# Decoding buffers moved to the memory that the global keys and values use later, and the decodings of the third block drawn together

## Chip, core and metric

One core of one Trainium2 chip runs the whole program. The time is device microseconds of one execution, and the span is what the profile shows from the first to the last instruction. The engines are named as the profile names them: PE (TensorE matmuls), PEld (its weight loads), DVE (VectorE), ACT (ScalarE), POOL (GpSimd) and SP (SyncE, which issues the transfers).

## What is computed

Attention with a local and a global part, then two feed-forward layers on the same 2304 tokens of width 512. Cut to what matters:

```python
s_g = scale * q_g @ k_all^T              # 32 global queries of a head see all 544 keys
out_g = softmax(s_g) @ v_all
s_l = scale * q_l @ [k_g, k_l]^T         # local: a window of 32 to each side, and the global keys
out_l = softmax(masked s_l) @ [v_g, v_l]
x = tokens of [out_g, out_l]             # 2304 x 512
x = elu(x @ w_in) @ w_out                # first layer, 512 -> 2048 -> 512
xn = x / rms(x) * rms_g                  # second layer, 512 -> 1536 -> 512
out = (silu(xn @ w_gate) * (xn @ w_val)) @ w_o2
```

The weights arrive as 64-bit floats. The kernel turns each word pair into a 32-bit float on ACT and DVE; this is what "decoding" means below.

## The kernel before

**Tiling.** The local tokens are four blocks of 512 (block 0 to block 3; the third block is block 2). `moe_block(b, slot)` runs the first layer for one block in 16 steps, j = 0 to 15. A step is `mm1` (12 matmuls into `h`, line 128), `act1` (ACT makes `e` from `h`, DVE finishes it, ACT copies a high part of `g`, line 135, and DVE makes its low part, line 136), and `mm2` for the `g` of the step before (12 matmuls into four `y`, line 142). `slot(j, part, h)` is called three times in a step and puts other work between the matmuls.

**Beside the steps of blocks 0 to 2** the local attention of the next block runs, one chunk of 128 tokens in four steps (`att_slot`): the scores `a_S` on PE (lines 209 to 219), the maximum `mx` on DVE (227) and the exponentials `E` on ACT (230), in the next step the transposes `a_T` (236), in the one after it `a_PV` (249) and `a_N`. The keys and queries of the next chunk (`load_kq`) are loaded once `a_S` has read the buffer, its values (`load_v`) once `a_PV` has.

**Decodings of the second layer's weights.** There are 18, each for 1 MiB of raw words. `w2_decode` (in part 2 of some steps of blocks 1 and 2) takes the oldest raw tile: ACT takes its absolute value into `dx` (line 79), DVE makes four passes over it (86 to 89), SP stores the result to `wT` in device memory (453), and `w2_load` (71) asks for the raw tile after next. There are two `raw` tiles (pool `decr`) and two `dx` tiles (pool `dec`). So decoding n waits for a load that is sent when decoding n-2 is done.

**Block 3** has the global attention beside it instead (`slot3`). `g_load_k(0)` loads the tile `gkq` (line 678, 1152 KB) and `g_load_v` two tiles `gvr` (685); `g_S` multiplies with them in step 0 (698), between `mm1` and `mm2`. Their pool is opened after the attention and decoding pools of blocks 0 to 2 have been closed and takes over their memory. In the kernel before, the two decoding pools are opened last in that group of pools (line 330).

**Order.** PE's order is the order of the code (`manual_schedule` for PE). A scheduler orders DVE, ACT and SP; each engine then runs its instructions in order, and a waiting instruction holds up all behind it on its engine.

Of the kernel before, what the change touches and what calls it, by code (L numbers as in the profile page):

```python
# [39 lines left out]
def fused_kernel(ctx: ExitStack, tc: tile.TileContext, kq, vl, gkq, gv, w_in, w_out, w_gate, w_val, w_o2, rms_g, consts, out):  # L40
# [91 lines left out]
    def act1(h, n, fn=None):  # L132
        e = (fn or elu)(h, n)
        g = moe.tile([P, 2, 512], F32R, tag="g", name="g", bufs=2)
        nc.scalar.copy(g[:, 0, :n], e[:, :n])  # L135
        nc.vector.tensor_tensor(out=g[:, 1, :n], in0=e[:, :n], in1=f(g[:, 0, :n]), op=ALU.subtract)  # L136
        return g
# [33 lines left out]


    with ExitStack() as ls:
        ac = ls.enter_context(tc.tile_pool(name="attc", bufs=1))
        ap_ = ls.enter_context(tc.tile_pool(name="attl", bufs=1))
        masks = ac.tile([P, 3, P], F32R, name="masks")
# [7 lines left out]
        def load_kq(u):  # L184
            if u < 16:
                if u < 4:
                    t = wpool.tile([P, 4, KC], F32, tag="w", name="kq0")
                else:
                    t = ap_.tile([P, 4, KC], F32, tag="kq", name="kq_")
                nc.sync.dma_start(out=t, in_=kq[u].rearrange("p (a n) -> p a n", a=4))  # L190
                kq_t[u] = t
# [87 lines left out]
        def att_slot(b, j, part):  # L279

            u, jj = 4 * (b + 1) + j // 4, j % 4
            if jj == 0 and part == 0:
                a_S(u, ATT2)
                a_E(u)
                load_kq(u + 1)
            if jj == 1 and part < 2:
                a_T(u, part, aps, "att")
            if jj == 2 and part == 0:
                a_PV(u, ATT2)
                a_N(u)  # L290
                load_v(u + 1)
# [35 lines left out]
            carry.append((ys, prev, t0, n))  # L327


        dec = {"t": ls.enter_context(tc.tile_pool(name="dec", bufs=2)), "r": ls.enter_context(tc.tile_pool(name="decr", bufs=2))}  # L330
        load_kq(0)
        mk = moe.tile([P, 3, P], F32, tag="e", name="mk", bufs=2)
        nc.sync.dma_start(out=ident, in_=consts[:, 3 * P:4 * P])
# [112 lines left out]
        def w2_decode():  # L446
            i = n_dec2[0]
            if i < 18:
                n_dec2[0] += 1
                raw = raws2.pop(0)  # L450
                t = dec_abs(dec["t"], raw, keep=True)
                dec_bits(t, raw)
                nc.sync.dma_start(out=wT[2 * i:2 * i + 2].rearrange("a p n -> p a n"), in_=t.rearrange("p (a n) -> p a n", a=2))
                w2_load()
# [15 lines left out]
        def slot12(b):  # L470
            def slot(j, part, h):
                g = act1(h, 512) if part == 0 else None
                att_slot(b, j, part)
                if part == 2:
                    if j % 2 or (b == 2 and j in (4, 10)):
                        w2_decode()
                return g

            return slot
# [429 lines left out]
```

## Time and profile before

| | us |
|---|---|
| median of 3 runs (lowest, highest) | 964.2 (962.63, 964.56) |
| the profiled execution's own time | 963.88 |
| its span | 962.1 |
| PE busy | 919.5 (96%) |
| DVE busy | 461.8 (48%) |
| ACT busy | 346.9 (36%) |
| DMA, mean over the span | 112 GB/s |

The page cuts the span into 40 slices and gives each engine's busy share of each. PE is at 90% or more in nearly all slices from the fifth on; the others are well below, DVE with its highest shares in the first third. The profiled execution stands 0.3 us under the median, so sums against its own time can be compared with the median as they are.

### The profile page before, as it was taken

Reading aid. Unit: us, or ns where it says so; the run is one execution under the profiler, and the core shown is the slowest. Engines: PE = TensorE matmul, PEld = TensorE weight load, DVE = VectorE, ACT = ScalarE, POOL = GpSimd, SP = SyncE. Lnnn points to the kernel's source line nnn. Section 1 sums busy time; section 2 is a strip of 40 time slices with the busy share of each in tenths; the row PEclk is TensorE's granted clock in tenths of the full one; section 3 lists DMA queues with packets and bytes.
Section 4 is the critical chain, followed back from the end, with each engine's and each line's share of the span. In section 5 each row is a group of like instructions: output and inputs, shape, how many; then the busy total and the mean of one; then the engine's idle time right before and its main releaser. Section 6 shows DMA issues by size and latency. Waiting matters only on the chain.

```text
span 962.1 us, 15714 instructions
## 1 busy us (share of the span) xinstructions
PE 919.5 (96%) x6738; PEld 769.7 (80%) x6738; DVE 461.8 (48%) x791; ACT 346.9 (36%) x627; POOL 17.9 (2%) x19
## 2 busy tenths in 40 slices
PE   6788899999999999599999999999999999999997
PEld 5666688888887887467788888888889999999996
DVE  4899953666656866434577313321332142141111
ACT  4566644433334344223465313121222232232111
POOL 0000000000000000000010100000000100100000
PEclk9989999999999999799999999999999999999999
DMA  9675441554465662533453200110011010000000
GB/s 362 243 293 197 171 163 45 185 176 173 170 240 179 233 244 89 218 133 131 183 171 111 77 0 1 33 44 1 1 33 44 1 33 33 1 1 33 1 1 33
DMA packets 34445, 107.77 MB, mean 112 GB/s; under 512 B 3016, under 2 KB 5704, under 8 KB 31816
## 3 DMA queue, kind: packets, MB, share of 16 engines
q1 hardware_dynamic: 34376, 106.77, 30.9%
q8 instruction: 53, 0.87, 0.4%
q14 instruction: 16, 0.13, 0.0%
HBM read 88.41 MB, written 18.35 MB: 111 GB/s over the span
## 4 chain that ended last, share of the span: by engine, by line
PE 82%; DVE 9%; DMA 3%; ACT 2%; issue 2%; SPq 0%; ACTq 0%; DVEq 0%
PE y L142 15%; PE pg L631 15%; PE pv L631 15%; PE y L637 15%; PE h L128 13%; DVE dx L89 2%; DVE dx L88 2%; PE ptp L236 2%; PE o L249 1%; PE yg L595 1%; PE s L219 1%; PE hg L579 1%; DMA kq<-in_kq 1%; PE s L214 1%; DVE wA L95 1%
## 5 line engine op out<-in xcount | busy, mean ns | idle before, releaser
L142 PE MATMUL y<-g,wA 128*128 128x512 f32 x768 | 201.4, 407 | 3.7 <-DVE g L136 3.4
L128 PE MATMUL h<-xT,wA 128*128 128x512 f32 x768 | 186.0, 391 | 1.3 <-DVE xT L274 1.3
L142 PEld LDWEIGHTS y<-g,wA 128*128 128x128 f32 x768 | 141.4, 192 | 37.3 <-DVE g L136 4.6
L128 PEld LDWEIGHTS h<-xT,wA 128*128 128x128 f32 x768 | 143.6, 188 | 31.9 <-DVE xT L274 1.5
L804 DVE TENSOR_TENSOR silu<-pv,silu 128x384 f32<-128x384 f32 (+1 forms) x60 | 36.6, 611 | 257.4 <-PE pv L631 251.3
L637 PE MATMUL y<-wB,p 128*128 128x512 f32 x612 | 149.0, 391 | 0.0
L637 PEld LDWEIGHTS y<-wB,p 128*128 128x128 f32 x612 | 114.5, 188 | 22.3
L803 ACT ACTIVATE silu<-pg 128x384 f32<-128x384 f32 (+1 forms) x60 | 32.0, 534 | 159.5 <-PE pg L631 159.3
L631 PE MATMUL pv<-xT,wB 128*128 128x384 f32 (+1 forms) x432 | 88.4, 353 | 0.0
L631 PEld LDWEIGHTS pv<-xT,wB 128*128 128x128 f32 x432 | 77.3, 188 | 5.6
L806 ACT CAST p<-silu 128x384 fp32r<-128x384 f32 (+1 forms) x60 | 33.3, 556 | 127.2 <-DVE silu L804 126.9
L135 ACT CAST g<-e 128x512 fp32r<-128x512 f32 x64 | 39.7, 621 | 72.6 <-DVE e L111 69.0
L109 ACT ACTIVATE e<-h 128x512 f32<-128x512 f32 x48 | 28.8, 600 | 94.8 <-PE h L128 87.5
L631 PE MATMUL pv<-xnB,wB 128*128 128x512 f32 (+1 forms) x288 | 61.5, 362 | 0.0
L631 PE MATMUL pg<-xT,wB 128*128 128x384 f32 (+1 forms) x288 | 60.1, 357 | 0.0
L631 PEld LDWEIGHTS pg<-xT,wB 128*128 128x128 f32 x288 | 52.2, 188 | 5.8 <-issue 0.5
L631 PEld LDWEIGHTS pv<-xnB,wB 128*128 128x128 f32 x288 | 52.2, 188 | 5.6
L110 DVE TENSOR_SCALAR e<-e 128x512 f32<-128x512 f32 x52 | 22.2, 428 | 70.9 <-ACT e L109 70.9
L807 DVE TENSOR_TENSOR p<-silu,p 128x384 fp32r<-128x384 f32 (+1 forms) x60 | 38.0, 633 | 35.5 <-ACT p L806 35.5
L136 DVE TENSOR_TENSOR g<-e,g 128x512 fp32r<-128x512 f32 x64 | 45.2, 706 | 17.4 <-ACT g L135 16.2
L79 ACT ACTIVATE dx<-raw 128x1024 f32<-128x1024 f32 x34 | 39.3, 1156 | 11.1 <-DVE wA L95 4.3
L230 ACT ACTIVATE E<-s,mx 128x128 f32<-128x128 f32 x128 | 34.9, 384 | 23.2 <-DVE mx L228 21.1
(179 smaller groups left out, 957.1 us busy)
## 6 DMA issues: line engine op xcount, KB each, us to landing
raw<-in_moe_w_out SPq DMA_DIRECT2D x14, 1024.0 KB, 5.3
wT<-dx SPq DMA_DIRECT2D x18, 512.0 KB, 3.9
wraw<-wT SPq DMA_DIRECT2D x18, 512.0 KB, 4.4
raw<-in_moe_w_in SPq DMA_DIRECT2D x8, 1024.0 KB, 7.0
raw<-in_moe_w_gate SPq DMA_DIRECT2D x6, 1024.0 KB, 7.8
raw<-in_moe_w_val SPq DMA_DIRECT2D x6, 1024.0 KB, 8.3
gvr<-in_gv SPq DMA_DIRECT2D x8, 640.0 KB, 4.5
gkq<-in_gkq SPq DMA_DIRECT2D x4, 1152.0 KB, 5.1
```

What stands on the lines that cost most here:

```text
L79: ins = nc.scalar.activation(x, f(words(raw)[:, :, 1]), AF.Abs)
L128: nc.tensor.matmul(h[:, :n], W1[c, G][:, ws, o:o + P], xT[c][:, xs, :n], start=(k == 0), stop=(k == 11))
L135: nc.scalar.copy(g[:, 0, :n], e[:, :n])
L136: nc.vector.tensor_tensor(out=g[:, 1, :n], in0=e[:, :n], in1=f(g[:, 0, :n]), op=ALU.subtract)
L142: nc.tensor.matmul(ys[dc][:, :n], W2[j][:, ws, dc * P:(dc + 1) * P], g[:, gs, :n], start=(j == 0 and k == 0), stop=(j == 15 and k == 2))
L230: nc.scalar.activation(e[par][:, pr, :], ss[par][:, pr, :], AF.Exp, bias=mx[:, par, pr:pr + 1], scale=SCALE)
L631: nc.tensor.matmul(ps[:, :n], W[c, G3][:, ws, o:o + P], xn[c][:, xs, :n], start=(k == 0), stop=(k == 11))
L637: nc.tensor.matmul(os_[t], p[:, pp, t * P:(t + 1) * P], Wo[j][:, ww, :], start=(j == 0 and k == 0), stop=(j == 11 and k == 2))
L803: nc.scalar.activation(s[:, :n], pg[:, :n], AF.Silu)
L804: nc.vector.tensor_tensor(out=s[:, :n], in0=pv[:, :n], in1=s[:, :n], op=ALU.mult)
L806: nc.scalar.copy(p[:, 0, :n], s[:, :n])
L807: nc.vector.tensor_tensor(out=p[:, 1, :n], in0=s[:, :n], in1=f(p[:, 0, :n]), op=ALU.subtract)
```

## The change

The pools of the decoding tiles are opened first in their group instead of last, so that the memory handed out first when the group is closed is theirs. In block 2, `w2_decode` is called in steps 0 to 4 and 6 to 10 instead of in the odd steps and in steps 4 and 10. Both make ten decodings in that block; block 1 stays as it was, with one in each odd step.

```diff
     with ExitStack() as ls:
+
+        dec = {"t": ls.enter_context(tc.tile_pool(name="dec", bufs=2)), "r": ls.enter_context(tc.tile_pool(name="decr", bufs=2))}
         ac = ls.enter_context(tc.tile_pool(name="attc", bufs=1))
...
-        dec = {"t": ls.enter_context(tc.tile_pool(name="dec", bufs=2)), "r": ls.enter_context(tc.tile_pool(name="decr", bufs=2))}
         load_kq(0)
...
                 if part == 2:
-                    if j % 2 or (b == 2 and j in (4, 10)):
+                    if (j % 2 if b == 1 else j < 12 and j % 6 != 5):
                         w2_decode()
```

PE's instructions keep their order. What moves stands on DVE, ACT and SP from the start of block 2 to the start of block 3. Lines 176 to 331 of the changed kernel are two lower than before and those behind them one lower, so that its 229, 230, 232 and 240 are the 227, 228, 230 and 238 of before.

DVE in step 4 of block 2, before. `e_3208` and `g_3212` belong to step 4, `mx_3259` to the chunk whose scores run in that step, `dx_3186` and `dx_3288` are decodings:

```order
L110 TENSOR_SCALAR e_3208<-e_3208 128x512
L89 SCALAR_TENSOR_TENSOR dx_3186<-raw_2912,dx_3186 128x1024
L111 SCALAR_TENSOR_TENSOR e_3208<-h_3195,e_3208 128x512
L227 TENSOR_REDUCE mx_3259<-s_3215 128x4
L136 TENSOR_TENSOR g_3212<-e_3208,g_3212 128x512
L227 TENSOR_REDUCE mx_3259<-s_3216 128x4
L228 TENSOR_SCALAR mx_3259<-mx_3259 128x4 x2
L86 TENSOR_SCALAR dx_3288<-dx_3288 128x1024
```

The same place after the change, where `e_3185` and `g_3189` belong to step 3, `e_3226` and `g_3230` to step 4, `dx_3163` and `dx_3204` to the decodings called in steps 2 and 3, and `mx_3277` to the same chunk:

```order
L89 SCALAR_TENSOR_TENSOR dx_3163<-raw_3030,dx_3163 128x1024
L111 SCALAR_TENSOR_TENSOR e_3185<-h_3172,e_3185 128x512
L136 TENSOR_TENSOR g_3189<-e_3185,g_3189 128x512
L86 TENSOR_SCALAR dx_3204<-dx_3204 128x1024
L87 TENSOR_SCALAR dx_3204<-dx_3204 128x1024
L110 TENSOR_SCALAR e_3226<-e_3226 128x512
L88 SCALAR_TENSOR_TENSOR dx_3204<-raw_3085,dx_3204 128x1024
L111 SCALAR_TENSOR_TENSOR e_3226<-h_3213,e_3226 128x512
L89 SCALAR_TENSOR_TENSOR dx_3204<-raw_3085,dx_3204 128x1024
L136 TENSOR_TENSOR g_3230<-e_3226,g_3230 128x512
L229 TENSOR_REDUCE mx_3277<-s_3233 128x4
```

Before, the first maximum stood ahead of `g` of its step; now a whole further decoding and the `g` stand ahead of both maxima.

ACT in steps 10 to 12 of block 2, before (`e_3713`, `e_3754` and `e_3845` are of steps 11, 12 and 13):

```order
L79 ACTIVATE dx_3691<-raw_3466 128x1024
L109 ACTIVATE e_3713<-h_3700 128x512
L135 CAST g_3717<-e_3713 128x512
L79 ACTIVATE dx_3732<-raw_3614 128x1024
L109 ACTIVATE e_3754<-h_3741 128x512
L135 CAST g_3758<-e_3754 128x512
```

And after (`e_3654`, `e_3736` and `e_3768` are of steps 10, 11 and 12):

```order
L79 ACTIVATE dx_3634<-raw_3484 128x1024
L135 CAST g_3605<-e_3601 128x512
L109 ACTIVATE e_3654<-h_3641 128x512
L135 CAST g_3658<-e_3654 128x512
L79 ACTIVATE dx_3716<-raw_3586 128x1024
L109 ACTIVATE e_3736<-h_3723 128x512
L135 CAST g_3740<-e_3736 128x512
L109 ACTIVATE e_3768<-h_3755 128x512
```

`dx_3716` is now the last decoding, ahead of the `e` of step 11, and none follows it; before, two more followed `dx_3732`, the last of them after step 15.

SP ahead of block 3, before:

```order
L71 DMA raw_3739<-in_moe2_w_out 128x2x512
L453 DMA wT_86<-dx_3878 128x2x512
L453 DMA wT_86<-dx_4022 128x2x512
L678 DMA gkq_4043<-in_gkq 128x2304
L685 DMA gvr_4045<-in_gv 128x1280
```

And after:

```order
L71 DMA raw_3586<-in_moe2_w_out 128x2x512
L202 DMA v__3702<-in_vl 128x2080
L454 DMA wT_86<-dx_3634 128x2x512
L454 DMA wT_86<-dx_3716 128x2x512
L679 DMA gkq_4043<-in_gkq 128x2304
```

The two stores ahead of `gkq` were those of the decodings called in steps 13 and 15 and are now those of steps 9 and 10.

## Rows read from the trace of the kernel before

**Rows 1.** The page, part 2: PE's busy tenths in 40 slices of the span.
```profile
PE   6788899999999999599999999999999999999997
```
**Rows 2.** Timeline of PE, end of block 2 and start of block 3: start us, us, instruction.
```profile
372.56 1.12 PE L249 MATMUL o<-v__3677,ET 128*32 128x65 f32 x64
...
384.37 2.88 PE L128 MATMUL h<-xT,wA 128*128 128x512 f32 x12
396.89 1.16 PE L698 MATMUL gs<-gkq 64*32 64x272 f32 x16 [9.64 <-DMA gkq<-in_gkq]
...
403.07 2.91 PE L128 MATMUL h<-xT,wA 128*128 128x512 f32 x12
...
410.59 3.02 PE L128 MATMUL h<-xT,wA 128*128 128x512 f32 x12
...
417.94 0.90 PE L729 MATMUL go<-gvr,gpt 128*32 128x64 f32 x40
```
**Rows 3.** The chain that ended last, from 340 to 400 us: start us, us, what.
```profile
388.79 2.71 DMA wT<-dx
391.65 5.11 DMA gkq<-in_gkq
```
**Rows 4.** Stretches: busy time of each engine, granted clock (PEclk), DMA share, GB/s.
```profile
117.90:121.30 3.40, 3.36 (x10) 2.79 (x11) 3.37 (x4) 3.01 (x8) 0.00 (x0) 0.50 0.67 276
...
396.80:401.20 4.40, 4.31 (x30) 2.31 (x38) 1.07 (x5) 0.59 (x1) 0.00 (x0) 0.50 0.57 238
```
**Rows 5.** Timeline of PE, at the wait before the first of those stretches.
```profile
117.94 1.12 PE L236 MATMUL ptp<-ident,E 128*128 128x128 f32 x4 [2.51 <-ACT E L230]
```
**Rows 6.** Timeline of PE, steps 4 to 6 of block 2.
```profile
301.84 2.88 PE L128 MATMUL h<-xT,wA 128*128 128x512 f32 x12
...
307.04 3.00 PE L142 MATMUL y<-g,wA 128*128 128x512 f32 x12
309.88 2.89 PE L128 MATMUL h<-xT,wA 128*128 128x512 f32 x12
312.61 0.60 PE L236 MATMUL ptp<-ident,E 128*128 128x128 f32 x4
...
316.26 2.88 PE L128 MATMUL h<-xT,wA 128*128 128x512 f32 x12
```
**Rows 7.** Timeline, steps 1 and 2 of block 2: ACT, DVE.
```profile
288.87 0.60 ACT L109 ACTIVATE e<-h 128x512 f32<-128x512 f32 x1 [4.35 <-DMA yT<-yev]
...
291.70 1.23 ACT L79 ACTIVATE dx<-raw 128x1024 f32<-128x1024 f32 x1
...
295.56 0.42 DVE L110 TENSOR_SCALAR e<-e 128x512 f32<-128x512 f32 x1
...
295.97 1.22 DVE L89 SCALAR_TENSOR_TENSOR dx<-raw,dx 128x1024 int32<-128x1024 int32 x1
...
298.47 0.69 DVE L136 TENSOR_TENSOR g<-e,g 128x512 fp32r<-128x512 f32 x1
```
**Rows 8.** Timeline of SP's queue, behind that last decode pass.
```profile
297.67 0.42 SPq L71 DMA_DIRECT2D raw<-in_moe_w_out  x1
```
**Rows 9.** Transfers issued near 297.7, 348.6 and 322.8 us: KB, us to landing.
```profile
raw<-in_moe_w_out SPq DMA_DIRECT2D x1, 1024.0 KB, 5.7
...
raw<-in_moe_w_val SPq DMA_DIRECT2D x1, 1024.0 KB, 8.5
...
raw<-in_moe_w_gate SPq DMA_DIRECT2D x1, 1024.0 KB, 9.1
```
**Rows 10.** Timeline of DVE and PEld, from a chunk's maxima to its transposes.
```profile
363.35 1.28 DVE L227 TENSOR_REDUCE mx<-s 128x4 f32<-128x512 f32 x2
...
366.00 0.42 PEld L236 LDWEIGHTS ptp<-ident,E 128*128 128x128 f32 x4 [0.54 <-ACT E L230]
```
**Rows 11.** Timeline, a decoding in a run of three: ACT's first pass, SP's store.
```profile
315.55 1.13 ACT L79 ACTIVATE dx<-raw 128x1024 f32<-128x1024 f32 x1
...
322.32 0.37 SPq L453 DMA_DIRECT2D wT<-dx  x1
```

## The prediction, made before the changed kernel was run

> **What bounds the kernel now.** I read the page's slices first, then PE's timeline round the slice that falls out, then the chain of waits there. PE is the bound: it is at 90% or more nearly everywhere after the first few slices, but one slice in the middle stands at 5 [rows 1]. The timeline names it: at the start of block 3 PE waits 9.64 us, with `gs`, for the load of `gkq` [rows 2]. `mm1` of step 0 starts at 384.37 and would be through 2.72 us later, as the other 12-matmul groups are (307.04 to 309.88 is one with its switch), but `gs` starts at 396.89, and step 1 only at 403.07 [rows 2, 6]. The chain says why: the store of the last decoding takes 2.71 us from 388.79, and the load behind it 5.11 us from 391.65 [rows 3]. So the load is late because the last decoding, called after step 15, has to be stored before its memory is free. After the wait PE works for 4.4 us at a granted clock of 0.50, that is at 1.2 of 2.4 GHz [rows 4].
>
> **What the change gives.** Step 0 of block 3 takes 403.07 - 384.37 = 18.70 us. Step 2 of that block has the same work up to its end (`mm1`, two `gs`, `mm2`) and takes 417.94 - 410.59 = 7.35 us without a wait [rows 2]. With `gkq` there in time the gain is 18.70 - 7.35 = **11.35 us**, the slow clock included.
>
> Will it be there? The last decoding is now called in step 10. The tiles of the attention still release memory and transfers late: the last to finish with its loads is `a_PV` of the last chunk, which starts at 372.56 before and ends a good microsecond later [rows 2]. A load issued at 374.1 that takes its 5.1 us [rows 3] is down at 379.2; PE asks at 384.37 + 2.72 = 387.1. The cover is 7.9 us, and a landing of 9.1, the longest of [rows 9], leaves 3.9. Both ends shift together if block 2 gets longer. The memory move alone could not do this while a decoding is called after step 15, and the earlier decodings alone leave the tiles of the attention in the way; I count the two as one edit.
>
> **What the change costs.** The ten decodings do not get cheaper; they come one per step. Their cover is the slack of ACT and DVE beside PE. A step of block 2 lasts (384.37 - 301.84) / 12 = 6.88 us over its last twelve [rows 2, 6]. Three places lose the cover, by the order of the instructions.
>
> *First, step 4.* The decoding of step 0 ends on DVE behind the first pass over `e` of step 1, and that `e` waits for a store of `yT` until 288.87 [rows 7]. With 0.60 us on ACT, 0.42 for that pass and 1.22 for the last decode pass [rows 7] it ends at 291.1; SP asks for the next raw tile 0.5 us after that pass, as at 297.67 [rows 8], at 291.6, with the value load of a chunk right behind it. Such a load took 5.7 us with only its store beside it, 8.5 with a value load and a store beside it, 9.1 with more [rows 9]. I take 8.5, which is the nearest case: 300.1. ACT has the pass over it ahead of `e` of step 3. From that pass to the end of the low part of `g` it takes 298.47 + 0.69 - 291.70 = 7.46 us [rows 7], so `g` is ready at 307.6. PE is through with `mm1` and the scores of step 4 5.20 us after its start [rows 6]. I put that start at 301.3, 0.5 us ahead of the 301.84 of before, since the decoding of step 0 no longer delays the `g` of step 2. Then `mm2` can start at 306.5, but its second matmul needs the low part at 307.6. It ends at 310.1, 0.3 us later than before.
>
> *Then step 5.* The next decoding starts on ACT when the high part of that `g` is made, 0.7 us before the low part, at 306.9, and lies ahead of `e` of step 4; DVE does all of it, and both passes of `g`, before the maxima of the scores. The same 7.46 us, less 0.6 since the last decode pass now fills the time that ACT needs for the high part, end at 313.8. From the maxima to PE's transposes it takes 366.00 - 363.35 = 2.65 us [rows 10], so the transposes start at 316.4. PE wants them 2.73 us into step 5 (312.61 - 309.88 [rows 6]), at 312.8, and waits 3.6 us. The step's rest is 316.26 - 312.61 = 3.65 us, and step 6 starts at 320.1 instead of 316.26: **3.8 us**. With a landing of 5.7 the first pass would go as soon as ACT is free, at 298.5, all is 1.6 us sooner and 2.3 us are lost; with 9.1 it is 4.4.
>
> *Step 12.* The last decoding is ahead of `e` of step 11, and its load is sent beside a value load and a store again. The trace shows no such case in these steps. With 5.7 us it hides; by the same chain of 7.46 us, 9.1 would cost 2.4. I take the middle, **1.2 us**, as the load is asked for beside the same neighbours as in step 4 but PE is 3.8 us later by then.
>
> *The clock.* A wait of PE of 2.51 us, for the same transposes, was followed by 3.4 us at 0.50 [rows 4, 5]. Such a stretch does half its work, 1.7 us less. A wait of 3.6 us in step 5 can bring one, that of step 12 another: 0 to 3.4 us. Part of it would be hidden by the waits that follow. I take half of one, **0.85 us**.
>
> *Gains of the same edit.* The decodings of steps 13 and 15 are gone, so the 0.54 us wait of the transposes in step 13 [rows 10] should shrink: -0.35 us, the difference to the other steps of its kind. The memset of block 3 and the store order cost nothing, since the stores they wait for were issued some 10 us before.
>
> **The sum.** 3.8 + 1.2 + 0.85 - 0.35 - 11.35 = -5.85. The profiled execution's own time is 963.88, so 958.0 us. Own range: all low, 2.3 + 0 + 0 - 0.35 - 11.35 = -9.4, gives 954.5; all high, 4.4 + 2.4 + 3.4 - 0.35 - 11.35 = -1.5, gives 962.4. The 963.88 is 0.3 us below the median of the runs, which I leave out.
>
> A rule that would move it: the Trainium skill, DMA: Bandwidth & Descriptors, section "Anatomy of one DMA", puts a transfer at a fixed 2.0 us and its bytes by 436 GB/s. By an estimate from it a raw tile of 1 MiB lands after 4.4 us, the first two places shrink to the low end and the third goes, which is 954.5. The rows say 5.7 to 9.1 [rows 9], and I follow them.
>
> **Rivals.**
>
> *The cover holds.* If the loads land in 5.7 us and DVE catches up before step 5, only the gain is left: 963.88 - 11.35 - 0.35 = 952.2, up to 954.5. For it: DVE is busy for less than half of the span and the ten decodings are the same work. Against it: the order puts a decoding ahead of the maxima whatever the loads do, and from there it takes 2.65 us [rows 10].
>
> *The two raw tiles set the pace (slower).* A decoding can't start before the load that was sent after the one before the last. In a run of decodings one took 322.32 - 315.55 = 6.77 us up to its store [rows 11], the load comes 0.5 later and takes up to 9.1 [rows 8, 9]: 16.4 us for two, 8.2 for each, against a step of 6.88. If that held for all eight loads that block 2 asks for, it would cost 8 x 1.3 = 10.5 us, with 3.6 for the transposes and 3.4 for the clock 17.5: 963.88 + 17.5 - 0.35 - 11.35 = 969.7. It makes the kernel slower from a cost of 13.3 us. Against it: 9.1 was one load among three [rows 9], and step 5 without a decoding lets the ring recover.
>
> *Gain and cost cancel.* The same mechanism at half its price, some 11 us: 962 to 966.
>
> *The change doesn't do what it says.* If `gkq` still waited for something late, the 9.6 us would stay with the cost on top: 963.88 + 5.5 = 969.4. The stores that stand ahead of it in SP's queue are now those of steps 9 and 10, which speaks against it.
>
> **How the numbers follow.** My sum has 0.70, the cover 0.12, the cancelling 0.09, slower by the raw tiles 0.07 and by a load that stays late 0.02. A difference under 0.2%, 1.9 us, can't be told from none, so same is 962.3 to 966.1. Nearly all of my own range and the first rival are faster, 0.81; same 0.10; slower 0.09. The range leaves out the lower half of the first rival (0.06), the slower cases (0.09) and a part of the cancelling ones (0.05): 953.5 to 963.5.
>
> **What would show it.** In the profile of the changed kernel the wait of `gs` for `gkq` should be gone and step 0 of block 3 should last 7.3 to 7.6 us, with the clock at 1.00. The load should be issued right behind the last `a_PV`, near 378, and land 5 to 6 us later. In block 2, PE should wait for `ACT E` in step 5 for 2 to 4 us, `mm2` for DVE's `g` in steps 4 and 12 for about a microsecond, and a stretch at 0.50 may follow. The first decode pass of ACT should show a wait for a raw tile near 300. I am wrong if those waits are absent (952), if ACT waits for a raw tile in most steps (over 966), or if `gs` still waits for a load.

## The result, and the profile after

The changed kernel takes **952.42 us** in the median of 4 runs (950.53 to 954.47); the kernel before, run beside it, 963.41 (962.55 to 964.56). The ratio is 0.9882 with a 95% interval of 0.9866 to 0.9899: 11.0 us faster, where 5.9 were forecast, and 1.1 us below the range. The direction was right, the size was not.

The profiled execution took 954.1 us, of which 952.2 are its span; against the 963.88 of the profile before that is -9.8. Of the page's 40 slices of PE, one stood at 5 before [rows 1]. It is gone:

```profile
PE   6789899999999999999999999999999999999997
```

PE's timeline where the last attention chunk ends and block 3 begins (start us, us, instruction; the counterpart of [rows 2]), and under it SP's queue at the same place:

```profile
374.28 1.12 PE L251 MATMUL o<-v__3702,ET 128*32 128x65 f32 x64
...
386.09 2.89 PE L128 MATMUL h<-xT,wA 128*128 128x512 f32 x12
388.90 0.69 PE L699 MATMUL gs<-gkq 64*32 64x272 f32 x16
...
393.22 2.90 PE L128 MATMUL h<-xT,wA 128*128 128x512 f32 x12
...
400.72 1.66 PE L128 MATMUL h<-xT,wA 128*128 128x512 f32 x6
```

```profile
350.97 8.14 SPq L454 DMA_DIRECT2D wT<-dx  x2
375.51 0.34 SPq L679 DMA_DIRECT2D gkq<-in_gkq  x1
375.90 0.90 SPq L686 DMA_DIRECT2D gvr<-in_gv  x2
```

`gs` no longer waits. Step 0 of block 3 lasts 393.22 - 386.09 = 7.13 us instead of 18.70. The last decoding's store is away by 359.1, and the load of `gkq` goes out 0.1 us behind the end of the last `a_PV` (374.28 + 1.12 = 375.40). It lands after 5.1 us, at 380.6, 8.3 us before PE uses it. The clock that fell after the wait before [rows 4] stays up; the stretch from 386 to 401 us reads, in the same columns:

```profile
386.00:401.00 15.00, 15.00 (x133) 10.98 (x132) 7.72 (x26) 6.14 (x12) 0.00 (x0) 1.00 0.47 150
```

What is left of the cost shows in PE's waits between 270 and 420 us (engine, line, what it waited for: us in total, times, longest). Before, the first line of this view was the 9.6 us for `gkq`:

```profile
PE ptp L238 <- ACT E L232: 1.7, 1, 1.7
PE xtp L274 <- DVE xT L276: 0.9, 2, 0.5
PE y L142 <- ACT g L135: 0.9, 1, 0.9
PE y L142 <- DVE g L136: 0.2, 1, 0.2
```

The 1.7 us are those of step 5, at the transposes, as forecast but half as long. Subtracting the starts of `mm1` gives the account of the two profiles. Here are those of steps 0, 5 and 6 of block 2 after the change, and of step 0 before:

```profile
273.87 2.89 PE L128 MATMUL h<-xT,wA 128*128 128x512 f32 x12
...
310.01 2.88 PE L128 MATMUL h<-xT,wA 128*128 128x512 f32 x12
...
318.31 2.88 PE L128 MATMUL h<-xT,wA 128*128 128x512 f32 x12
```

```profile
273.18 2.89 PE L128 MATMUL h<-xT,wA 128*128 128x512 f32 x12
```

| | forecast, us | measured, us |
|---|---|---|
| step 0 of block 3 | -11.35 | 7.13 - 18.70 = -11.57 |
| steps 0 to 5 of block 2, with the wait in step 5 | +3.8 | 44.44 - 43.08 = +1.36 |
| step 12 | +1.2 | 8.06 - 8.04 = +0.02 |
| slow clock behind those waits | +0.85 | 0 |
| step 13 | -0.35 | 6.38 - 6.72 = -0.34 |
| **sum** | **-5.85** | **-10.53** |

The other 0.75 us lie outside: block 2 begins 0.69 us later in this profile, where the first keys at 14 us were waited for 1.45 us instead of 0.68, and 0.06 us are left for the rest. Of the steps 0 to 5, step 5 alone is +1.92 (8.30 instead of 6.38). Steps 2 and 3 are -0.60 together, but that is no effect of the change: a kernel with the old steps, below, has them as short.

### The profile page after: what moved, and what is told of

It reads as the page before. It is cut to its first block, busy times and chain, and to the rows that moved or that the text cites. A ratio compares the mean times of both kernels' runs of the same rounds, so it can differ in the third digit from the quotient of the medians.

```text
span 952.2 us, 15710 instructions
## 1 busy us (share of the span) xinstructions
PE 917.5 (96%) x6738; PEld 768.5 (81%) x6738; DVE 460.5 (48%) x791; ACT 347.1 (36%) x627; POOL 17.9 (2%) x19
## 4 chain that ended last, share of the span: by engine, by line
PE 85%; DVE 9%; DMA 2%; ACT 2%; issue 1%; SPq 0%; ACTq 0%; DVEq 0%
PE y L142 16%; PE pg L632 15%; PE pv L632 15%; PE y L638 15%; PE h L128 15%; DVE dx L89 1%; DVE dx L88 1%; PE o L251 1%; PE ptp L238 1%; PE yg L596 1%; DMA kq<-in_kq 1%; PE s L221 1%; PE hg L580 1%; PE s L216 1%; DVE mx L229 1%
## 5 line engine op out<-in xcount | busy, mean ns | idle before, releaser
(179 smaller groups left out, 954.5 us busy)
```

## The experiments

The changed kernel was run again as a measure, twice.

> The changed kernel once more, as the measure for the runs beside it. Both theories: 950 to 955 us, 10 to 12 us under the kernel before; PE waits 1.7 us for E in step 5 of block 2 and not at all for gkq.

> The changed kernel itself, beside gap4_A_2 on the same chip: 951 to 953 us, with the wait of 1.5 to 1.7 us in step 5.

Measured: 951.82 us (950.87 to 954.19, 5 runs; ratio 0.9889, 0.9869 to 0.9909) and 952.62 us (952.10 to 953.95, 4 runs; 0.9892, 0.9875 to 0.9910). The wait in step 5 is 1.54 us in both; `gs` doesn't wait.

### The two edits apart

The steps alone, with the pools left last:

```diff
-                    if j % 2 or (b == 2 and j in (4, 10)):
+                    if (j % 2 if b == 1 else j < 12 and j % 6 != 5):
```

> The ten decodings in steps 0 to 4 and 6 to 10, the two decoding pools opened last as before. Theory A, the steps alone make the gain, since the load of gkq waits for all the tiles of the group wherever the pools lie: the same as the changed kernel, 950 to 955 us, no wait for gkq. Theory B, which the prediction took when it counted both as one edit, the steps alone leave the tiles of the attention in the way: the load of gkq goes out later than the 375.5 us of the changed kernel by the time that those tiles stay in use, and if it goes out more than 8 us later a wait of gs for gkq is back and the time lies between 953 and 964 us.

Measured: **952.57 us** (951.25 to 952.87, 5 runs; 0.9889, 0.9872 to 0.9907). Its PE and its SP, where the last chunk ends:

```profile
373.04 1.12 PE L249 MATMUL o<-v__3702,ET 128*32 128x65 f32 x64
...
387.66 0.69 PE L698 MATMUL gs<-gkq 64*32 64x272 f32 x16
```

```profile
374.26 0.35 SPq L678 DMA_DIRECT2D gkq<-in_gkq  x1
```

The load again leaves 0.1 us behind the end of `a_PV` (374.16). The memory alone, with the old steps:

> The pools opened first, the decodings in their old steps. Both theories: no gain, since the last decoding is still called after step 15: 962 to 965 us, gs waits 9 to 10 us for gkq. If the memory alone helped, the load of gkq would go out right behind the last a_PV near 375 and the time would fall to 952 to 954 us.

Measured: **962.72 us** (10 runs; 1.0001, 0.9989 to 1.0012), and this wait:

```profile
PE gs L699 <- DMA gkq<-in_gkq: 9.7, 1, 9.7
```

Theory A holds: the steps are the whole gain, and the place of the pools is worth nothing. In both layouts the load leaves behind the last user of the closed group: the last `a_PV` in the changed kernel and in order_only, the store of the last decoding in the kernel before and here. The runs do not show whose memory it took over. This run also has the old order of DVE and ACT in block 2, and yet its steps 2 and 3 last 6.70 and 5.86 us where the profile before has 7.70 and 6.54: those two steps vary by themselves.

### How late a decoding may be called

One decoding of the old steps moved, from step 15 to step 12. The pools are opened first, so the diff is against the kernel move_only:

```diff
-                    if j % 2 or (b == 2 and j in (4, 10)):
+                    if (j % 2 if b == 1 else j in (1, 3, 4, 5, 7, 9, 10, 11, 12, 13)):
```

> The old steps of the decodings with one of them moved: 1, 3, 4, 5, 7, 9, 10, 11, 12 and 13, so only the decoding after step 15 is called earlier, after step 12. Theory A, the whole gain comes from that one decoding: its store leaves near step 14, the load of gkq behind it is down before PE asks, no wait of gs, and as no decoding stands ahead of the maxima in step 4 there is no wait of 1.7 us in step 5 either: 949.5 to 952 us, no slower than the changed kernel. Theory B, the decodings have to end well before the last a_PV in step 14: two more decodings behind step 11 make the load late again, a wait of gs of 1 to 5 us, 952 to 957 us.

Measured: **951.81 us** (950.43 to 952.44, 4 runs; 0.9878, 0.9861 to 0.9894), no wait for `gkq`, no wait in step 5. Theory A: moving that one decoding brings as much as moving all ten.

The last decoding after step 14, the others as in the next experiment (steps 0, 1, 2, 4, 5, 6, 8, 9, 10 and 14):

> As gap4_A, with the last decoding after step 14 instead of step 12. In the kernel before, the store of the decoding of step 13 left 12.2 us after the start of that step. By the same way this store leaves 12.2 us after the start of step 14, the load of gkq 2.7 us behind that and lands 5.1 us later, 20.0 us after the start of step 14; PE asks for it 17.4 us after that start. Theory A: gs waits 2 to 4 us. Theory B, the cover that the prediction worked out for the last a_PV holds for this too: no wait.

Measured, in a single run: 952.39 us, and

```profile
386.55 0.69 PE L699 MATMUL gs<-gkq 64*32 64x272 f32 x16 [1.09 <-DMA gkq<-in_gkq]
```

```profile
353.67 25.11 SPq L454 DMA_DIRECT2D wT<-dx  x2
381.26 0.35 SPq L679 DMA_DIRECT2D gkq<-in_gkq  x1
```

The wait is back, as theory A says, but with 1.1 us instead of 2 to 4: the store, the second in the row, left 10.5 us after the start of step 14 (at 367.94) rather than 12.2. The cover ends between a last call in step 13 and one in step 14.

### What makes the wait in step 5

No decoding in steps 3, 7 and 11, the last in step 12:

```diff
-                    if (j % 2 if b == 1 else j < 12 and j % 6 != 5):
+                    if (j % 2 if b == 1 else j < 13 and j % 4 != 3):
```

> The changed kernel with the ten decodings of block 2 in steps 0, 1, 2, 4, 5, 6, 8, 9, 10 and 12. On DVE no decoding stands between the g of step 3 and the maxima of step 4 any more. Theory A, the wait of 1.7 us in step 5 comes from the decoding of step 3 that is ahead of the maxima: that wait goes and block 2 is 1.5 to 2 us shorter, 948.5 to 953 us, 1.5 to 2 us under the changed kernel of the same chip. Theory B, it comes from ten decodings in too few steps whatever stands ahead of the maxima: the wait stays within 0.5 us of 1.7 and the time is that of the changed kernel. In both the load of gkq is still there in time, since the last decoding is called in step 12 and the last a_PV runs in step 14.

> gap4_A once more, beside the changed kernel on the same chip: 949 to 951 us, 1.5 to 2.5 us under the changed kernel.

Measured: **949.77 us** (948.76 to 951.42, 5 runs; 0.9870, 0.9849 to 0.9890) and **949.76 us** (947.89 to 951.84, 5 runs; 0.9864, 0.9843 to 0.9885), 2.1 and 2.9 us under the changed kernel on the same chips. The wait in step 5, 1.54 us in both of those, is gone; what else there is was not taken apart, and step 2, which varies by itself, is part of it. The reason for the wait is on DVE. In the changed kernel, from the `g` of step 3 to the maxima (L229) of step 4:

```profile
304.93 0.69 DVE L136 TENSOR_TENSOR g<-e,g 128x512 fp32r<-128x512 f32 x1 [0.69 <-ACT g L135]
306.81 0.69 DVE L86 TENSOR_SCALAR dx<-dx 128x1024 f32<-128x1024 f32 x1 [1.19 <-ACT dx L79]
...
310.22 1.22 DVE L89 SCALAR_TENSOR_TENSOR dx<-raw,dx 128x1024 int32<-128x1024 int32 x1
311.35 0.68 DVE L136 TENSOR_TENSOR g<-e,g 128x512 fp32r<-128x512 f32 x1
311.95 1.28 DVE L229 TENSOR_REDUCE mx<-s 128x4 f32<-128x512 f32 x2
```

In gap4_A the same stretch has no decoding in it:

```profile
301.69 0.69 DVE L136 TENSOR_TENSOR g<-e,g 128x512 fp32r<-128x512 f32 x1 [0.69 <-ACT g L135]
...
304.13 0.69 DVE L136 TENSOR_TENSOR g<-e,g 128x512 fp32r<-128x512 f32 x1 [0.69 <-ACT g L135]
304.74 1.28 DVE L229 TENSOR_REDUCE mx<-s 128x4 f32<-128x512 f32 x2
```

From the `g` of step 3 to the maxima it takes 7.02 us in the first and 3.05 in the second, and there PE takes its transposes without a wait:

```profile
309.38 0.60 PE L238 MATMUL ptp<-ident,E 128*128 128x128 f32 x4
```

The other way round, decodings in step 3, 7 and 11 and none in 4 and 8 (steps 0 to 3, 5 to 7 and 9 to 11):

> The changed kernel with the ten decodings of block 2 in steps 0, 1, 2, 3, 5, 6, 7, 9, 10 and 11: the decoding of step 3 still stands ahead of the maxima of step 4, none is called in step 4. Theory A, the decoding of step 3 makes the wait in step 5: 1.3 to 2 us, as in the changed kernel. Theory B, the one of step 4 makes it, or five in a row do: the wait goes.

Measured, in a single run: 954.79 us. PE's waits of this kind between 300 and 370 us:

```profile
313.45 0.66 PE L238 MATMUL ptp<-ident,E 128*128 128x128 f32 x4 [1.80 <-ACT E L232]
340.68 0.66 PE L238 MATMUL ptp<-ident,E 128*128 128x128 f32 x4 [0.43 <-ACT E L232]
368.47 0.66 PE L238 MATMUL ptp<-ident,E 128*128 128x128 f32 x4 [0.98 <-ACT E L232]
```

They are in steps 5, 9 and 13: here there is one behind each decoding that was called in the step before the scores. That is theory A, and the first stays even without a decoding in step 4. The place alone does not make the wait, though. In the changed kernel the decoding of step 7 stands in the same place, and in one_early those of steps 3, 7 and 11. Here are the transposes of step 9 in the first, then the only ones that waited in the second, those of step 13:

```profile
341.24 0.60 PE L238 MATMUL ptp<-ident,E 128*128 128x128 f32 x4
```

```profile
365.13 0.66 PE L238 MATMUL ptp<-ident,E 128*128 128x128 f32 x4 [0.30 <-ACT E L232]
```

In all profiles the wait follows a decoding of step 3, 7 or 11 of block 2 where each of the two steps before it had a decoding too (0.3 to 1.8 us, and 3.95 in max_thrice), and not where only one or none had. In one_early, DVE takes the maxima of the chunk of step 4 from 306.48 to 308.55, before step 5 begins at 308.83; in the changed kernel it starts on them 1.9 us after that step's start (311.95 against 310.01). No run tests this condition by itself.

As gap4_A, with the decoding of step 0 moved to step 13:

> As gap4_A, with the decoding of step 0 moved to step 13: steps 1, 2, 4, 5, 6, 8, 9, 10, 12 and 13. Theory A: no wait of gs, none in step 5, and the short wait for g in step 2 goes too: 948.5 to 951.5 us, within 0.5 us of gap4_A. Theory B: the load of gkq comes late, 1 to 5 us more than gap4_A.

Measured: 950.46 us (949.20 to 952.05, 4 runs; 0.9867, 0.9852 to 0.9881), no wait for `gkq` or in step 5: not to be told from gap4_A. A decoding may be called in step 13 still. Short waits for `g` and `ET` of 0.2 to 0.8 us were in steps 2 and 3 this time.

### The landing of a raw tile

In the changed kernel the load after the decoding of step 0 goes out 0.5 us ahead of a value load. Here it is sent behind it:

```diff
+        def r2_load(b, j, part):
+            with tc.issue_after(v_dma[0].ins): w2_load() if b == 2 and j == 2 and part != 1 else None
...
-                att_slot(b, j, part)
+                att_slot(b, j, part); r2_load(b, j, part)
...
-                        w2_decode()
+                        w2_decode(not (b == 2 and j < 2))
```

(`w2_decode(False)` leaves its own `w2_load` out, so that the loads of the decodings of steps 0 and 1 are both called in step 2; `v_dma[0]` is the last value load. The second of them still goes out behind the store of the decoding of step 1.)

> The changed kernel with the raw tile that is asked for after the decoding of step 0 of block 2 sent behind the value load of its step instead of ahead of it; the next raw tile goes out behind the store of the decoding of step 1, as before. Of the other engines' order ACT's and DVE's passes over this tile move one place back, so the run is for the landing, not for the time. Theory A, a load pays for what was sent ahead of it and not for what was sent behind: this load, which landed 5.6 us after its issue with the value load behind it, takes 8 to 9.5 us, as the two loads of the kernel before that were sent 1.8 and 2.5 us behind a value load (8.5 and 9.1), and ACT's first pass waits for it. Theory B, as the prediction took it, a neighbour costs the same on either side: the same landing as in the changed kernel, 5.5 to 6.5 us.

Measured, in a single run, first the loads of the changed kernel issued at 292.28 and 292.80, then those of this one, issued at 292.19 (raw) and 291.68 (values); KB, us to landing:

```profile
v__3149<-in_vl SPq DMA_DIRECT2D x1, 1040.0 KB, 8.9
raw<-in_moe_w_out SPq DMA_DIRECT2D x1, 1024.0 KB, 5.6
```

```profile
v__3145<-in_vl SPq DMA_DIRECT2D x1, 1040.0 KB, 5.8
raw<-in_moe_w_out SPq DMA_DIRECT2D x1, 1024.0 KB, 9.3
```

The two loads change places and their times with them. ACT's first pass now waits for the tile:

```profile
301.61 1.12 ACT L79 ACTIVATE dx<-raw 128x1024 f32<-128x1024 f32 x1 [2.17 <-DMA raw<-in_moe_w_out]
```

Theory A, on this one pair: a load pays for what was sent ahead of it. The Trainium skill, DMA: Bandwidth & Descriptors, section "Queues, rings and completion order", says that each engine of a queue takes its descriptors in the order of its ring, and these two pairs of rows agree. The prediction had left the order out. The whole took 953.09 us, and PE's wait in step 5 was 1.36 us, no longer than in the changed kernel although ACT began on the tile 3.3 us later (301.61 against 298.33): ACT and DVE do their passes in another order around this tile. So this run is for the landing only, and no run delays the landing alone to show what that does to the wait.

### What the forecast wait would have cost

Each of the two maxima of the chunk in step 4 taken three times:

```diff
-                nc.vector.tensor_reduce(out=mx[:, par, :], in_=ss[par], axis=AX.X, op=ALU.max)
+                [nc.vector.tensor_reduce(out=mx[:, par, :], in_=ss[par], axis=AX.X, op=ALU.max) for _ in range(3 if u == 13 else 1)]
```

> The changed kernel, with each of the two maxima of the chunk whose scores run in step 4 taken three times, so that DVE's result comes 4 x 0.64 = 2.6 us later and nothing that stands ahead of it moves. The wait for E in step 5 grows from 1.6 to about 4.2 us, more than the 3.6 us of the prediction. Theory A, as the prediction priced it: a stretch at half clock of about 3.4 us follows and costs some 1.7 us more: 4.3 us over the changed kernel, 956 to 957 us. Theory B: the clock stays at 1.00 and only the wait is paid: 2.6 us over it, 954 to 955 us.

Measured: 955.62 us (954.66 to 956.77, 4 runs; 0.9920, 0.9905 to 0.9935), which lies between the two ranges. The profile decides. Step 5, as PE sees it, with the granted clock (the first of the last three numbers) behind the wait:

```profile
306.79 2.88 PE L128 MATMUL h<-xT,wA 128*128 128x512 f32 x12
313.62 0.66 PE L238 MATMUL ptp<-ident,E 128*128 128x128 f32 x4 [3.95 <-ACT E L232]
314.03 2.64 PE L142 MATMUL y<-g,wA 128*128 128x512 f32 x6
...
318.92 1.32 PE L128 MATMUL h<-xT,wA 128*128 128x512 f32 x5
```

```profile
313.60:317.00 3.40, 3.38 (x13) 2.74 (x14) 1.34 (x3) 2.99 (x7) 0.00 (x0) 0.61 0.52 216
```

The first half of `mm2`, 6 matmuls, takes 2.64 us instead of the 1.64 of the changed kernel, and the granted clock is 0.61 in the mean of those 3.4 us. Behind the shorter wait of the changed kernel it is 1.00:

```profile
314.50:318.30 3.80, 3.70 (x20) 3.15 (x21) 1.65 (x4) 3.53 (x9) 0.00 (x0) 1.00 1.01 394
```

The step lasts 12.13 us, 3.83 more than the 8.30 of the changed kernel. The wait grew by 3.95 - 1.71 = 2.24, so 1.6 us are the clock. Theory A, in this profile: behind the wait of 3.95 us the clock fell, behind that of 1.71 us it did not.

## Why the prediction was wrong

*The gain* was right to 0.2 us: the reading of the slice, the timeline and the chain [rows 1 to 3], the step without the wait, and that `gkq` would be there. The load left right behind the last `a_PV`, as forecast, but at 375.5 and not near 378, since block 2 lost less than forecast; the cover is 8.3 us (forecast 7.9).

*That the two edits count as one* was wrong. The steps alone do all of it, and "the earlier decodings alone leave the tiles of the attention in the way" holds for both layouts alike: in both the load leaves behind `a_PV`, and in both that is early enough. It cost nothing in the sum. It would have cost a reader who kept the memory move for its gain.

*The step that failed is the landing in step 4.* The sentence "I take 8.5, which is the nearest case: 300.1." took a row by its neighbours and not by their order. The 9.1 and 8.5 of [rows 9] are loads that were sent 2.5 and 1.75 us behind a value load, as SP's queue in the kernel before shows:

```profile
320.25 0.34 SPq L200 DMA_DIRECT2D v__3413<-in_vl  x1
...
322.78 0.42 SPq L71 DMA_DIRECT2D raw<-in_moe_w_gate  x1
...
346.81 0.34 SPq L200 DMA_DIRECT2D v__3677<-in_vl  x1
...
348.56 0.42 SPq L71 DMA_DIRECT2D raw<-in_moe_w_val  x1
```

The load in question goes out 0.5 us ahead of one and took 5.6. The experiment with the order turned round gave 9.3. From there the forecast chain holds nearly to the tenth. From the first pass to the end of the low part of `g` it takes 305.62 - 298.33 = 7.29 us (7.46), and from the maxima to the transposes 314.60 - 311.95 = 2.65 (2.65). With `g` 2.0 us earlier than forecast, the maxima are 1.85 earlier and the wait is 1.71 instead of 3.6. The prediction's own branch for a landing of 5.7 had 2.3 us lost, and step 5 became 1.92 longer. `mm2` of step 4, which was to wait for the low part of `g`, did not wait. The wait in step 5 doesn't vanish: the next tile was sent while the value load was still in flight, ACT could start on it 8.0 us later (297.65 to 305.64), and it waited 0.74 for it. The forecast had not priced this second load. The 4.4 us that the prediction estimated from the Trainium skill, DMA: Bandwidth & Descriptors, section "Anatomy of one DMA", were too short by 1.2 us. That section gives its figures for transfers that GpSimd issues, and these loads are issued by SP, which the prediction didn't say; they were still nearer to the 5.6 than the 8.5 that was taken.

*Step 12* was the same error once more: its load went 2.1 us ahead of a value load, landed in 6.6 us and hid; ACT waited 1.1 us for it and PE not at all. *The slow clock* was priced rightly for a wait of this length (1.7 against 1.6 measured in max_thrice), but that wait didn't come. *Step 13* was right. Of the 4.68 us between the two sums of the account, 2.44 are the landing in step 4 and what follows up to step 5 (0.56 of them by other steps than step 5, which vary by themselves), 1.18 step 12, 0.85 the clock and 0.22 the gain.

Two figures of the working are a little off, and nothing hangs on them. The example for the 2.72 us of `mm1`, 307.04 to 309.88, is an `mm2` and gives 2.84; 309.88 to 312.61 gives 2.73. The cost of 13.3 us that makes the kernel slower leaves out the 0.35 gained in step 13.

*The range.* All terms at their low end gave 954.5, and the profiled execution took 954.1. The range missed by 1.1 because its lower end cut through the rival "the cover holds" (952.2, with a chance of 0.12), which is what came about but for the wait of 1.7 us. That the profile after stands 1.7 us above its own median did the rest.

Left open is why the wait is 0.43 to 1.80 us behind decodings that all stand at the same place of a chunk and follow two others (gap4_B); the loads of each differ, but this was not taken apart.

## To carry to other kernels

When one load stalls the start of a phase, look for the last user of anything in the memory group it is put into: here one decoding moved by three steps brought the whole gain, and the place of the buffers none. When work is packed closer, keep it out of the step before a chain that PE will wait for (maxima, exponentials, transposes), at least where the steps before that one hold such work too: with those steps free this kernel was 2 to 3 us faster, of which the wait is 1.5. Take the price of a transfer from a row with the same work ahead of it in the queue; a load sent 0.5 us behind cost this one nothing that shows (5.6 us with it, 5.7 without).

## What the runs showed of the hardware

The clock does not fall behind the same wait every time. All fourteen profiles have a wait of 2.3 to 2.5 us for `E` near 117 us, ahead of block 2. In eleven of them the granted clock from 114 to 124 us is 0.83 in the mean; in gap4_A, gap4_B and max_thrice it is 1.00. Here are that wait and that stretch in the changed kernel, and then in gap4_A:

```profile
118.61 0.97 PE L238 MATMUL ptp<-ident,E 128*128 128x128 f32 x4 [2.51 <-ACT E L232]
114.00:124.00 10.00, 7.49 (x31) 5.85 (x30) 9.36 (x14) 8.22 (x16) 0.00 (x0) 0.83 0.67 222
```

```profile
117.08 0.66 PE L238 MATMUL ptp<-ident,E 128*128 128x128 f32 x4 [2.51 <-ACT E L232]
114.00:124.00 10.00, 7.49 (x62) 5.74 (x64) 9.26 (x13) 8.88 (x18) 0.00 (x0) 1.00 0.64 218
```

The same wait, and the transposes behind it at either speed. The stretch costs less here than the 1.7 us that half a clock for 3.4 us would make. The step with the wait and the step behind it last 17.2 to 17.4 us together with the stretch, and 16.5 to 16.7 without it. So it costs 0.5 to 0.9 us; in gap4_A, PE waits for `g` in the second step instead. Executions of one kernel lie up to 5 us apart, and such stretches can be part of it; what decides whether one comes was not found.
